# Decode attention on one core: scores and maxima by unit instead of by pair, and two more kept loads

## The chip, the cores and the metric

The kernel runs on one core of a Trainium2 chip. The core has a matrix engine (PE, with its weight loads listed apart as PEld), a vector engine (DVE), a scalar engine (ACT), GpSimd (POOL) and a sync engine (SP), which here issues nearly all DMAs. The engines run their own instruction lists in order and wait for each other on semaphores. The metric is the device time of one execution in microseconds.

## The reference

Two layers run twice over one token for each of four batches: attention over a cache of 4096 keys, then a gated feed-forward layer.

```python
x = x + A(layernorm(x))   # attention
x = x + B(layernorm(x))   # gated feed-forward
x = x + A(layernorm(x))   # the same weights and caches again
x = x + B(layernorm(x))

# A: q = x @ wq, 32 heads of 128; 8 key/value heads, each shared by 4 query heads
scores = q . k * 128**-0.5          # [4, 32, 1, 4096]
o = softmax(scores) . v
A = o.reshape(4, 1, 4096) @ wo      # to 512
# B: (sigmoid(x @ w_gate) * (x @ w_up)) @ w_down, F = 1792
```

All inputs are bfloat16. K and V are 4 x 8 blocks of 4096 x 128, 1.0486 MB each, 64 blocks in all, and both attention passes read all of them.

## The kernel before

A *unit* is one layer, batch and key/value head: 64 units, and each needs its K and its V block. Two units next to each other in head number make a *pair*, 32 in all. ORDER lists the pairs (layer, batch, pair of heads). Batches go their own way: when a batch's four pairs of layer 0 are done, its feed-forward and its next query are computed in a *pass* of 17 short steps (pass_steps), spread between the work on other batches' pairs.

Blocks live in 12 slots of SBUF; the four quarters of wq become slots 13 to 16 once the last query is made. KEPT names, per batch, the units whose K (ahead of the slash) and V (behind it) stay in their slots from layer 0 to layer 1. All others are loaded twice. Before, 27 blocks are kept, so 101 K and V loads remain of 128. LOADS is the order in which SP issues the loads (k, v, and the weight parts o, g, u, d). The function pump issues the next load whenever a slot is free on the list; SP's DMA then waits for the last reader of that slot.

PROGRAM is the order of all other work, written out by hand, a letter for each step. The letters that matter here, for pair g:

- t, T: turn half or all of a K block in place on DVE (k_turn, L1014)
- b: POOL copies the pair's queries into qz (q_blocks, L728)
- s, z: the scores on PE (scores, L1016 to L1040), in two parts
- m: maxima over each row on DVE (smax, L1049)
- p: PE spreads the row maxima to all rows (spread_max, L1057)
- n: DVE picks each row's own maximum (bias, L1068)
- e: the exponential on ACT (expo, L1080); h: POOL splits the sums in a high and a low half (L1109, L1112)
- P: PE transposes the probabilities (ptrans, L1098); C, D: eight copies to pT, on ACT (L1150; for the last pair half on DVE, L1142)
- r, i: row sums on PE (L1164) and their reciprocals on DVE (L1176)
- a: half a unit's PV product (pv, L1196); the second half gives the V slot back
- o, N: normalise (L1227); w: product with wo (L1253, L1279 or L1346)
- x: a row sum of one wo part on ACT (wo_row_sums, L602); X, Y: the last layer norm's preparation (Y is rows_before, L1393)
- a dot: the next step of the pass of a batch

Each engine's list has the steps in this order, so a step whose input is late holds up everything behind it on that engine. A pair's scores lie in one PSUM bank of 128 rows by 512 columns. The array's four strips of 32 output rows each take one of two units and one of two halves of the keys:

```python
r0 = 64 * ul + 32 * c
S_ps[p][r0:r0 + 4 * REP, :]   # ul: unit of the pair, c: half
rhs=ktv[ul][:, :, c, :, b2, :, e_]   # 512 columns
```

Part s has the first two of four contraction steps t for both units, part z the other two; both K slots go back after z.

Of the kernel before, what the change touches and what calls it, by code (L numbers as in the profile page):

```python
# [5 lines left out]
dt = mybir.dt  # L6
ACTF = mybir.ActivationFunctionType
ALU = mybir.AluOpType
# [126 lines left out]
stzxaamatbpaoCnwfitaDTaewFl sazamhrPpCoDwnei.....w..Ph..r.aa...aa.oiC.Daa..b sxTzmpnaebaTowtPChr  # L135
sziampnbDatweaahtPr sCzobimDaap snzaamewhPCobp swtrznftehwiDrtFabalmaaotwxtPp
sxinw.zCmbaTp.eD.w.ha.TnaaPo. sCDrz.iawTePbma..hpa.aCnTo.r..DiT sz.aw.bmae.P.apaohDrtw
swinCewahazPabmapC strznoeiamwpbhnDaParaoiC sDewfaazFPhlaarwmpConiwaDtt.aTehabPawoC.DTri.
swz.w..mawa.ap.baTn soezhrimP.p.bTCa.Daw.nt.aa.. se.ztw.Pbw smzCphnoribDtweaPtmaahpaC
snerzmDoiaaTpaabhnwTP sCorzwwettwbiaDaawmpTPhaCDr sToinzbmepwahPanraaTC  # L140
sDwoeziambPpahaaroCnDiwteahfrFtaalaPDoiw.T.CTaa. szmw...pb.Tn.eaa.
shzr.oPwwDiw..C.matpwa.n.eP..tabTa shzDomCbrpnei szahmawPaTrbaCp snDoizmaehabPapawrCtw
stonzmbwiapTDenhPaa sDraozeCiaPhamCrapaDnowwefihFPDCaaaalorXaaYiNawa
# [3 lines left out]
def bass_interleave_layers__gqa_block_cached__glu_gated_glu__decode_kernel(  # L147
# [60 lines left out]
    valid_p = wide_sb[:, 0:NV]  # L208
    pe_sb = wide_sb[:, NV:NV + 4 * P]
    mask_f = wide_sb[:, NV + 4 * P:2 * NV + 4 * P].rearrange("p (n w) -> p n w", n=8)  # L210
# [4 lines left out]
    pT_sb = sbt([P, 2, 4, 2, 4, REP], dt.bfloat16, "pT")  # L215
    NSMALL = 87
# [20 lines left out]
    rm_bf = small(2, dtype=dt.bfloat16)[:, 0:1]  # L237
    hl_bf = small(2, dtype=dt.bfloat16)
    head_bf = small(2 * REP, dtype=dt.bfloat16)
    eye4 = small(Bn)  # L240
    sel_bf = small(Bn, dtype=dt.bfloat16)
    sm_sb = small(1)
    nm_sb = small(1)
    head_f = small(2 * REP)
# [24 lines left out]
    ident_f = t_row[:, 0:P]  # L269
    half_f = t_row[:, P:P + 8 * REP].rearrange("p (u w) -> p u w", u=2)  # L270
# [164 lines left out]
    act(lambda e: e.activation(ident_f[:, :], ident_bf[:, :], ACTF.Copy), reads=IDENT, writes=["ra"])  # L435
    rows_f = ident_f.rearrange("p (u c w) -> p u c w", u=2, c=2)
# [4 lines left out]
    def head_masks():  # L441
        for u in range(2):
            dve(
                (lambda u: lambda e: e.tensor_copy(
                    valid_p.rearrange("p (c a u h) -> p u c a h", c=2, a=4, u=2)[:, u],
                    rows_f[:, u, :, 0:4 * REP].rearrange("p c (a h) -> p c a h", h=REP),
                ))(u),
                reads=["ra"],
                writes=[f"valid{u}"],
            )  # L450
        dve(
            lambda e: e.tensor_tensor(
                half_f[:, :, :], rows_f[:, :, 0, 0:4 * REP], rows_f[:, :, 1, 0:4 * REP], ALU.add
            ),
# [3 lines left out]
            lambda e: e.tensor_reduce(  # L458
                head_f.rearrange("p (u h) -> p u h", u=2),
                half_f.rearrange("p u (a h) -> p u h a", h=REP),  # L460
                AX.X,
                ALU.add,
            ),
# [13 lines left out]
        dve(lambda e: e.tensor_copy(sel_bf, eye4), reads=["eye4"], writes=["sel"])  # L477
        dve(
            lambda e: e.tensor_scalar(
                mask_f, head_f.unsqueeze(1).broadcast_to([P, 8, 2 * REP]), 1.0, BIG, op0=ALU.subtract, op1=ALU.mult  # L480
            ),
            reads=["head"],
            writes=["mask"],
        )
        dve(lambda e: e.tensor_reduce(rm_sb, head_f, AX.X, ALU.add), reads=["head"], writes=["rm"])
# [530 lines left out]
    def scores(g, part):  # L1016
        l, b, _ = seq[2 * g]
        p = g % 2
        ktv, rd = [], list(QZ)
        for ul in range(2):  # L1020
            st = where["kt", b, seq[2 * g + ul][2]]
            ktv.append(slot[st].rearrange("p (x c j t k e) -> p x c j t k e", x=XJ, c=2, j=4, t=2, e=2))
            rd.append(f"s{st}")
        fns = []
        for t in range(2 * part, 2 * part + 2):
            b2, e_ = divmod(t, 2)
            for ul in range(2):
                for c in range(2):
                    r0 = 64 * ul + 32 * c
                    fns.append(  # L1030
                        (lambda t, b2, e_, c, r0, ul: lambda e: e.matmul(  # L1031
                            S_ps[p][r0:r0 + 4 * REP, :],
                            lhsT=qz_sb[:, ul, t, :, :].rearrange("p a r -> p (a r)"),
                            rhs=ktv[ul][:, :, c, :, b2, :, e_].rearrange("p x j k -> p j x k"),
                            start=(t == 0),
                            stop=(t == NT4 - 1),
                        ))(t, b2, e_, c, r0, ul)
                    )
        if part == 0:
            S.group("pe", fns, reads=rd, writes=[f"S{p}"])  # L1040
            return
        S.last_write[f"S{p}"] = S.group("pe", fns, reads=rd)
# [10 lines left out]
    def spread_max(g, n):  # L1053
        ms_bank[0] = n
        S.inst(
            "pe",
            lambda e: e.matmul(  # L1057
                O_ps[n][:, 128:128 + 16 * REP], lhsT=rm_bf.broadcast_to([P, P]), rhs=valid_p[:, :],
                start=True, stop=True,
            ),  # L1060
            reads=["rmb", "valid0", "valid1"],
            writes=[f"O{n}"],
        )

    def bias(g):
        n = ms_bank[0]
        dve(
            lambda e: e.tensor_tensor_reduce(  # L1068
                O_ps[n][:, 256:256 + 16 * REP], O_ps[n][:, 128:128 + 16 * REP],
                mask_f.rearrange("p n w -> p (n w)"),  # L1070
                rowk_f, BIG, ALU.add, ALU.min, nm_sb,
            ),
            reads=["mask", "rowk"],
            writes=[f"O{n}", "nm"],
        )

    def expo(g):
        p = g % 2
        act(
            lambda e: e.activation(  # L1080
                pe_sb,
                S_ps[p][:, :],
                ACTF.Exp,
                bias=nm_sb,
                scale=exp_scale,
                accum_out=sm_sb,
            ),
            reads=[f"S{p}", "nm"],
            writes=["pe0", "sm"],
        )  # L1090
# [591 lines left out]
```

## Time and profile before

| What | Before |
|---|---|
| Median of 3 runs | 310.94 us (310.31 to 311.24) |
| Profiled execution, its own time | 309.33 us |
| Its span, first to last instruction | 307.3 us |
| Busy: PE, PE weight loads, DVE, ACT, POOL | 219.4, 130.2, 183.7, 107.3, 40.6 us |
| Mean granted TensorE clock | 0.684 |
| Read from HBM | 119.80 MB, 390 GB/s over the span |
| K and V loads | 101 blocks, one of them in two halves |
| Stream transposes of K (L1014) | 103.8 us on DVE in the main slots |
| Scores (L1031) | 496 + 16 matmuls, 60.9 + 2.1 us |
| PV (L1196), main group | 1824 matmuls, 60.2 us |

The profile page divides the span in 40 slices of 7.7 us and gives the busy share of each engine in tenths. Rows by line give busy time, mean time of one instruction, and the idle time ahead of it with what ended it. The chain of waits goes back from the last instruction to what released it at each step.

### The profile page before, as it was taken

What the parts mean: (1) busy time and instruction counts of PE and PEld (TensorE: products, weight loads), DVE (VectorE), ACT (ScalarE), POOL (GpSimd) and SP (SyncE); (2) the same over time, 40 slices, a digit from 0 to 9 for tenths busy, and PEclk for the clock granted to TensorE, in tenths of its full rate; (3) what the DMA queues carried; (4) which work ended last, traced back from release to release, by engine and by line L of the source; (5) the groups of instructions that cost most, each with busy time, mean ns of one, the idle gap of its engine ahead of it and who ended that gap; (6) DMA issues with size and microseconds to landing.
All of it is one profiled execution on the core that took longest, in us unless ns stands there. A gap on an engine that the chain in (4) does not pass through costs nothing.

```text
span 307.3 us, 10060 instructions
## 1 busy us (share of the span) xinstructions
PE 219.4 (71%) x4264; PEld 130.2 (42%) x4264; DVE 183.7 (60%) x407; ACT 107.3 (35%) x350; POOL 40.6 (13%) x205
## 2 busy tenths in 40 slices
PE   1223334544889699798979987965965689799986
PEld 1221112212545343556445735443433645355575
DVE  6345665437333767686933586766974496767333
ACT  2001123134213254624345632343555204446700
POOL 0002110101000212111111020131112010222000
PEclk9999999999995555557655557575755575555555
DMA  7999999999999999999999999999999999999940
GB/s 278 424 398 403 403 410 399 412 422 421 397 409 419 414 401 395 424 417 419 419 416 405 422 419 419 419 420 419 419 421 416 422 361 358 423 424 418 420 166 5
DMA packets 20788, 120.45 MB, mean 392 GB/s; under 512 B 1924, under 2 KB 6024, under 8 KB 7688
## 3 DMA queue, kind: packets, MB, share of 16 engines
q1 hardware_dynamic: 20720, 119.81, 95.8%
q8 instruction: 34, 0.56, 0.7%
q14 instruction: 10, 0.08, 0.1%
q10 hardware_dynamic: 24, 0.01, 0.0%
HBM read 119.80 MB, written 0.00 MB: 390 GB/s over the span
## 4 chain that ended last, share of the span: by engine, by line
DMA 41%; PE 33%; DVE 12%; SPq 5%; issue 4%; ACT 2%; POOL 1%; DVEq 0%; ACTq 0%; POOLq 0%
DMA slot<-in_A_v_cache_dram 33%; PE S_ps L1031 10%; PE O_ps L1196 9%; DMA slot<-in_A_k_cache_dram 8%; DVE slot L1014 7%; SPq L372 5%; PE M_ps L904 4%; PE PT L1098 2%; DVE small L1049 1%; ACT pT L1150 1%; PE AC L1253 1%; POOL qz L728 1%; PE M_ps L953 1%; PE M_ps L504 1%; PE O_ps L1346 1%
## 5 line engine op out<-in xcount | busy, mean ns | idle before, releaser
L1014 DVE STREAM_TRANSPOSE slot<-slot 128x1024 f32<-128x1024 f32 (+1 forms) x61 | 103.8, 1707 | 22.5 <-DMA slot<-in_A_k_cache_dram 20.1
L1150 ACT ACTIVATE pT<-PT 32x128 bf16<-32x128 f32 x236 | 63.3, 268 | 78.2 <-PE PT L1098 34.6
L1196 PEld LDWEIGHTS O_ps<-pT,slot 128*128 128x128 bf16 x1824 | 55.5, 104 | 50.1 <-DMA slot<-in_A_v_cache_dram 15.5
L1196 PE MATMUL O_ps<-pT,slot 128*128 128x4 bf16 x1824 | 60.2, 166 | 22.3 <-DMA slot<-in_A_v_cache_dram 14.5
L1031 PE MATMUL S_ps<-slot,qz 128*16 128x512 bf16 x496 | 60.9, 610 | 18.7 <-DVE slot L1014 11.3
L728 POOL COPY qz<-qs 32x32 bf16<-32x32 bf16 x128 | 26.2, 205 | 123.3 <-PE S_ps L1031 65.6
L1049 DVE TENSOR_REDUCE small<-S_ps 128x1 bf16<-128x512 f32 x32 | 21.8, 681 | 25.1 <-PE S_ps L1031 25.1
L1080 ACT ACTIVATE wide<-S_ps,small 128x512 bf16<-128x512 f32 x32 | 22.0, 687 | 38.7 <-DVE small L1068 21.5
L1031 PEld LDWEIGHTS S_ps<-slot,qz 128*16 128x16 bf16 x496 | 11.1, 102 | 36.1 <-DVE slot L1014 13.8
L1098 PE MATMUL PT<-ident_bf,wide 128*128 128x64 bf16 (+1 forms) x288 | 18.3, 225 | 2.9 <-ACT pT L1150 2.9
L1098 PEld LDWEIGHTS PT<-ident_bf,wide 128*128 128x128 bf16 x288 | 14.9, 120 | 8.2 <-ACT pT L1150 3.0
L1109 POOL CAST small<-small 128x1 bf16<-128x1 f32 x32 | 6.0, 187 | 80.9 <-ACT wide L1080 66.7
L904 PE MATMUL M_ps<-wq,small 128*1 128x512 bf16 x128 | 15.5, 602 | 0.0
L1068 DVE CUSTOM_DVE_ANT_0 O_ps<-O_ps,wide,small 128x64 f32<-128x64 f32 x32 | 8.9, 278 | 9.2 <-PE O_ps L1057 5.1
L1057 PE MATMUL O_ps<-wide,small 128*128 128x64 bf16 x32 | 7.1, 221 | 10.1 <-DVE small L1049 9.7
L1227 DVE TENSOR_TENSOR oT<-O_ps,small 128x8 bf16<-128x8 f32 (+1 forms) x32 | 5.3, 164 | 14.7 <-PE O_ps L1196 12.3
L1253 PE MATMUL AC<-wo,oT 128*1 128x512 bf16 x96 | 12.0, 596 | 0.8 <-DVE oT L1227 0.8
L713 ACT ACTIVATE qs<-M_ps 128x128 bf16<-128x128 f32 x8 | 1.9, 280 | 27.2 <-PE M_ps L702 27.2
L1057 PEld LDWEIGHTS O_ps<-wide,small 128*128 128x128 bf16 x32 | 3.3, 104 | 16.4 <-DVE small L1049 15.8
L1164 PEld LDWEIGHTS O_ps<-small 128*128 128x128 bf16 x62 | 4.2, 109 | 12.0 <-issue 6.0
L858 PE MATMUL M_ps<-wu,small 128*1 128x512 bf16 (+1 forms) x64 | 8.9, 522 | 0.0
L919 ACT ACTIVATE t_row<-M_ps,small 128x512 bf16<-128x512 f32 x4 | 2.7, 687 | 15.6 <-PE M_ps L904 8.4
(143 smaller groups left out, 204.9 us busy)
## 6 DMA issues: line engine op xcount, KB each, us to landing
slot<-in_A_v_cache_dram SPq DMA_DIRECT2D x52, 1024.0 KB, 9.9
slot<-in_A_k_cache_dram SPq DMA_DIRECT2D x44, 1024.0 KB, 10.5
wq<-in_A_wq_dram SPq DMA_DIRECT2D x2, 2048.0 KB, 10.2
wo<-in_A_wo_dram SPq DMA_DIRECT2D x8, 512.0 KB, 17.6
wq<-in_A_v_cache_dram SPq DMA_DIRECT2D x2, 1024.0 KB, 10.3
wq<-in_A_k_cache_dram SPq DMA_DIRECT2D x2, 1024.0 KB, 14.4
wg<-in_B_w_gate_dram SPq DMA_DIRECT2D x2, 896.0 KB, 14.6
wu<-in_B_w_up_dram SPq DMA_DIRECT2D x2, 896.0 KB, 13.3
```

The costliest lines, as they stand in the source:

```text
L372: "sp", (lambda dst, frm: lambda e: e.dma_start(dst, frm))(dst, frm), sem, writes=[key], deps=deps
L728: (lambda a, ps: lambda e: e.tensor_copy(qz_sb[ps, :, :, a, :], qs_sb[b][ps, :, u * REP:(u + 2) * REP].rearrange("p t (u r) -> p u t r", r ...
L904: (lambda k, st: lambda e: e.matmul(M_ps[h][32 * st:32 * st + 1, :], lhsT=xc_bf[:, k, 0:1], rhs=wv[:, k, h, :, st, :], start=(k == 0), sto ...
L1014: dve(lambda e: e.transpose(kf, kf), writes=[f"s{st}"])
L1031: (lambda t, b2, e_, c, r0, ul: lambda e: e.matmul(S_ps[p][r0:r0 + 4 * REP, :], lhsT=qz_sb[:, ul, t, :, :].rearrange("p a r -> p (a r)"), ...
L1049: dve(lambda e: e.tensor_reduce(rm_bf, S_ps[p][:, :], AX.X, ALU.max), reads=[f"S{p}"], writes=["rmb"])
L1057: lambda e: e.matmul(O_ps[n][:, 128:128 + 16 * REP], lhsT=rm_bf.broadcast_to([P, P]), rhs=valid_p[:, :], start=True, stop=True,),
L1080: lambda e: e.activation(pe_sb, S_ps[p][:, :], ACTF.Exp, bias=nm_sb, scale=exp_scale, accum_out=sm_sb,),
L1098: (lambda w, a0, a1, c0: lambda e: e.matmul(PT[:, c0:c0 + 16 * (a1 - a0)], lhsT=wide_sb[:, NV + 64 * w:NV + 64 * w + P], rhs=valid_bf[:, : ...
L1150: (lambda dst, frm: lambda e: e.activation(dst, frm, ACTF.Copy))(dst, frm),
L1196: (lambda n, x, c, j: lambda e: e.matmul(bank[:, ul * REP:(ul + 1) * REP], lhsT=vv[:, x * JG + c * 4 + j, :], rhs=pT[:, x % 2, j, x // 2, ...
L1253: (lambda r, h, i: lambda e: e.matmul(AC[32 * r:32 * r + 1, :], lhsT=oT_sb[:, h, own_column:own_column + 1], rhs=wo_sb[:, h, :], start=(j ...
```

## The change

- The score matmuls go unit by unit. The four strips take four quarters of one unit's keys (c and x1), the bank's left 256 columns are the first unit and the right 256 the second. Part s is now all of the first unit, part z all of the second: 16 matmuls of 256 columns each, where each part had 8 of 512.
- A K slot is given back after its own unit's part.
- Each row's maxima, exponentials and sums are made per unit: one reduction with two results, two spreading matmuls, a scalar_tensor_tensor and a minimum reduction in place of one fused operation, two exponentials of 256 columns, four row-sum matmuls for two.
- The masks that serve these are built another way at the start (head_masks), and the layouts of pT and small tiles follow.
- KEPT has 29 blocks, and ORDER, LOADS and PROGRAM are written anew.

```diff
-KEPT = ["012345/23", "0145/45", "167/167", "23567/26"]
+KEPT = ["012345/23", "0145/01", "167/0167", "23567/236"]
 ORDER = """
-000 002 001 003 011 013 101 010 012 100 102 022 021 020 023 112 110 103 030 032 123 120 033 031 113
-111 121 133 131 130 132 122
+002 000 003 001 013 011 101 012 010 100 102 022 021 020 023 110 112 030 103 032 123 120 033 031 111
+113 121 131 133 130 132 122
 """
 LOADS = """
-vkkookokgk kookkvovko vgkkvvkvvo uuddvvvkvk kkvvkvvkvk kvvkvkkvvk vvvvvvkkkk vvvkvkvkvk kvvkkkvkvv
-kvvkvkkvkv kvkvvvkkvv vvvvv
+ookokokkvk koovvkkgkk vkovvkovvg uuddvvvkkv kkkvvvvkvk kvvkvkvkvk vvvvvvkkvk vkvvkkkvkv kvvkkkvkvv
+vkkvvkkvvv kvkkkvkvvv vvv
 """
 PROGRAM = """
-tw szmpnbetT szhrmTbiTPwpDn sezhCttmaaptaatnrPCoiDb seazmhpwtabrawPwntaehotDCPwir
...
-stonzmbwiapTDenhPaa sDraozeCiaPhamCrapaDnowwefihFPDCaaaalorXaaYiNawa
+stzbmpntt szxmethxwTptb strPiCznaDaeaaoPmxwpDnhrCTTib swazemhaaaoPrttbpTDwniC
...
+saCDareoiPzhaaramaCpwDonewfiFaPwwahCwlaXYaarDoiawNawa
 """
...
     def scores(g, part):
-        l, b, _ = seq[2 * g]
+        l, b, u = seq[2 * g + part]
...
+        half = slice(256 * part, 256 * part + 256)
         fns = []
-        for t in range(2 * part, 2 * part + 2):
+        for t in range(NT4):
             b2, e_ = divmod(t, 2)
-            for ul in range(2):
-                for c in range(2):
-                    r0 = 64 * ul + 32 * c
+            for c in range(2):
+                for x1 in range(2):
+                    r0 = 64 * c + 32 * x1
...
-                            S_ps[p][r0:r0 + 4 * REP, :],
-                            lhsT=qz_sb[:, ul, t, :, :].rearrange("p a r -> p (a r)"),
-                            rhs=ktv[ul][:, :, c, :, b2, :, e_].rearrange("p x j k -> p j x k"),
+                            S_ps[p][r0:r0 + 4 * REP, half],
+                            lhsT=qz_sb[:, part, t, :, :].rearrange("p a r -> p (a r)"),
+                            rhs=ktv[:, 2 * x1:2 * x1 + 2, c, :, b2, :, e_].rearrange("p x j k -> p j x k"),
...
-        for i in (2 * g, 2 * g + 1):
-            if l == 1 or not kept("k", i):
-                free.append(where.pop(("kt", b, seq[i][2])))
+        if l == 1 or not kept("k", 2 * g + part):
+            free.append(where.pop(("kt", b, u)))
 
     def smax(g):
-        dve(lambda e: e.tensor_reduce(rm_bf, S_ps[p][:, :], AX.X, ALU.max), reads=[f"S{p}"], writes=["rmb"])
+        dve(lambda e: e.tensor_reduce(rm_bf, S_ps[p].rearrange("p (u n) -> p u n", u=2), AX.X, ALU.max), reads=[f"S{p}"], writes=["rmb"])
...
     def spread_max(g, n):
-            lambda e: e.matmul(
-                O_ps[n][:, 128:128 + 16 * REP], lhsT=rm_bf.broadcast_to([P, P]), rhs=valid_p[:, :],
+                (lambda u: lambda e: e.matmul(
+                    O_ps[n][:, P + 64 * u:P + 64 * u + 64], lhsT=rm_bf[:, u:u + 1].broadcast_to([P, P]), rhs=valid_bf,
...
     def bias(g):
-            lambda e: e.tensor_tensor_reduce(
-                O_ps[n][:, 256:256 + 16 * REP], O_ps[n][:, 128:128 + 16 * REP],
-                mask_f.rearrange("p n w -> p (n w)"),
-                rowk_f, BIG, ALU.add, ALU.min, nm_sb,
+            lambda e: e.scalar_tensor_tensor(
+                out=shifted, in0=maxima, scalar=rowk_f, in1=mask_f.rearrange("p n w -> p (n w)").unsqueeze(1).broadcast_to([P, 2, 64]),
+                op0=ALU.mult, op1=ALU.add,
...
+        dve(lambda e: e.tensor_reduce(nm_sb, shifted, AX.X, ALU.min), reads=[f"O{n}"], writes=["nm"])
 
     def expo(g):
-                pe_sb,
-                S_ps[p][:, :],
+        for u in range(2):
+                    pe_sb[:, half],
+                    S_ps[p][:, half],
...
     def row_sums(g):
-                    bank[:, 16:16 + 2 * REP], lhsT=hl_bf[:, n:n + 1].broadcast_to([P, P]), rhs=head_bf,
+                    bank[:, 16 + u * REP:16 + (u + 1) * REP], lhsT=hl_bf[:, n, u:u + 1].broadcast_to([P, P]), rhs=head_bf,
```

More of the change, by code (lines that the diff above doesn't have):

```diff
@@ L1054, in spread_max @@
         ms_bank[0] = n
[L1055 removed]
+        S.group(
             "pe",
[L1057 to L1061 removed]
+            [
+                (lambda u: lambda e: e.matmul(
+                    O_ps[n][:, P + 64 * u:P + 64 * u + 64], lhsT=rm_bf[:, u:u + 1].broadcast_to([P, P]), rhs=valid_bf,
+                    start=True, stop=True,
+                ))(u)
+                for u in range(2)
+            ],
+            reads=["rmb"] + IDENT,
             writes=[f"O{n}"],
```

126 lines of the change are left out of this document (54 added, 72 removed).

## The prediction

> **What bounds the kernel now.** I read the page's 40 slices first, then the queues, then busy time and DMA rate stretch by stretch, then the chain of waits, and last the rows of the operations that the diff touches.
>
> ```profile
> PE   1223334544889699798979987965965689799986
> DMA  7999999999999999999999999999999999999940
> GB/s 278 424 398 403 403 410 399 412 422 421 397 409 419 414 401 395 424 417 419 419 416 405 422 419 419 419 420 419 419 421 416 422 361 358 423 424 418 420 166 5
> q1 hardware_dynamic: 20720, 119.81, 95.8%
> DMA 41%; PE 33%; DVE 12%; SPq 5%; issue 4%; ACT 2%; POOL 1%; DVEq 0%; ACTq 0%; POOLq 0%
> ```
>
> The DMA engines are full from the first slice to the 38th, near 420 GB/s, and stop about 12 us before the end. PE fills nine tenths of many slices in the second half too, so it is the second limit.
>
> ```profile
> 112.00:120.00 8.00, 7.96 (x146) 4.38 (x147) 4.05 (x9) 3.47 (x13) 2.12 (x11) 0.50 0.97 376
> 164.00:168.00 4.00, 4.00 (x92) 2.67 (x92) 1.20 (x5) 2.27 (x8) 1.20 (x6) 0.50 0.99 399
> 244.00:252.00 8.00, 6.20 (x87) 3.27 (x87) 7.33 (x14) 1.34 (x4) 1.06 (x5) 0.65 0.95 365
> 256.00:260.00 4.00, 3.79 (x39) 1.83 (x31) 2.09 (x13) 2.08 (x8) 0.31 (x2) 0.50 0.88 309
> ...
> 266.40:292.20 25.80, 23.82 (x452) 13.34 (x452) 15.82 (x33) 15.87 (x54) 5.57 (x29) 0.50 1.01 421
> ```
>
> Columns: stretch, length, busy PE, PE weight loads, DVE, ACT, POOL, granted clock, DMA share, GB/s. In the first four rows compute is late in giving slots back and the queue runs short. Against 420 GB/s they lose (44x8 + 21x4 + 55x8 + 111x4)/420 = 3.1 us. In the last row the queue is full while PE idles 2.0 us of 25.8.
>
> ```profile
> 228.38 12.18 DMA slot<-in_A_v_cache_dram
> ...
> 240.61 0.59 PE O_ps L1196 x16
> ...
> 272.38 22.35 DMA slot<-in_A_v_cache_dram
> ...
> 294.87 0.99 PE O_ps L1196 x32
> 295.86 0.60 PE S_ps L1393 x16
> ```
>
> This is the chain in order of time (start, length). It ends on the last V loads: all are queued by 275, the last lands at 294.7, and 12.4 us of compute follow. So the end is bytes over rate, plus a tail.
>
> **The change, part by part.**
>
> *Two loads fewer.* The kept lists hold 27 units before and 29 after (a V each of batches 2 and 3 more), so 101 K and V loads become 99. A load is 1.0486 MB: at 420 GB/s 2.50 us, together **-5.0 us**. Where in the list? Counted from the two load lists, 22 loads stand behind the last layer-0 V in both. The saving lies ahead of it, so the last batch's pass (its serial feed-forward and query, which that V releases: 240.6 to about 266 here) may start 5 us earlier, and what follows has the same length. That matters since PE has only 2.0 us to spare behind the pass. The gain holds if compute ahead of it keeps up: from 104 to 244 PE is busy 115.9 of 140 us, and 24 idle minus 5 leaves 19. Bounds 0 and -5.0; I take -5.0.
>
> *Slots given back.* A K slot now goes back after its own unit's scores, not the pair's; but more kept units leave fewer slots in circulation. I walked both programs through the slot count, taking for each load the bytes between it and the newest load that the steps up to its release need. The smallest distance was 1.0 MB before, at the first of the loads that are issued from 246 to 257 us, with others of 2.1. After, the smallest is 2.1 MB (5.0 us); between them stand mostly 3.1 to 5.2 MB in both. Bounds: all 3.1 us recovered, or as much lost again if steps lie otherwise than counted; nearer to a small gain, **-0.5 us**.
>
> *Scores.* Sixteen matmuls of 512 columns per pair, in four strips, become 32 of 256.
>
> ```profile
> L1031 PE MATMUL S_ps<-slot,qz 128*16 128x512 bf16 x496 | 60.9, 610 | 18.7 <-DVE slot L1014 11.3 <-POOL qz L728 4.4 <-DVE oT L1227 1.8
> L833 PE MATMUL M_ps<-wg,small 128*1 128x256 bf16 x16 | 4.5, 408 | 0.0
> L1608 PE MATMUL S_ps<-wd,t_row 128*4 128x128 bf16 x56 | 1.7, 309 | 0.2 <-DVE t_row L785 0.2
> L1068 DVE CUSTOM_DVE_ANT_0 O_ps<-O_ps,wide,small 128x64 f32<-128x64 f32 x32 | 8.9, 278 | 9.2 <-PE O_ps L1057 5.1 <-ACT slot L1150 1.7 <-PE O_ps L1164 1.6
> L1068 DVE DVE_READ_ACCUMULATOR2_ANT small<- 128x1 f32 x32 | 4.5, 141 | 0.0
> L1080 ACT ACTIVATE wide<-S_ps,small 128x512 bf16<-128x512 f32 x32 | 22.0, 687 | 38.7 <-DVE small L1068 21.5 <-PE PT L1098 6.9 <-issue 5.2
> L1080 ACT ACTIVATION_READ_ACCUMULATOR wide<-S_ps,small 128x1 f32 x32 | 6.2, 193 | 0.0
> ```
>
> A sequence of 16 takes 1.89 us: four sets of four strips at a pitch of (1.89-0.61)/3 = 0.43 us. The only four-strip row with narrower matmuls, L1608 (128 columns), has (1.69-0.31)/13 = 0.106 us per set. That is a quarter, so pitch goes with columns: 256 take 0.21, and eight sets 7x0.21 + 0.41 = 1.88 us. Bounds: 0 per pair, and +1.71 if a set of 256 takes as long as one of 512. I take 0, by the L1608 row.
> The Trainium skill speaks against the split: "TensorEngine Tiling (Array Packing)", section Instruction Overhead, gives each matmul about 60 cycles on trn2; at 1.2 GHz ("TensorE: Matmul & The Clock Gate", What's actually happening) an estimate of 50 ns, 0.8 us more per pair if it adds. L1608's 30 ns per matmul disagrees with an addition; as a floor it doesn't bind.
>
> *Softmax chain, per pair.* The fused bias operation (0.28, its accumulator read ending 0.35 us after the start) becomes a scalar_tensor_tensor over 128 columns (between 168 ns at 4 columns and 688 at 512: 0.29) and a minimum (158 and 681: 0.29). With a gap of 0.05 that is +0.28. The exponential becomes two of 256 columns (between 280 ns at 128 and 687 at 512: 0.42), each with a 0.19 read: 1.22 for 0.88, +0.34. A second max-spreading matmul is 0.05, by nine transposes in 0.45. Together +0.67 us. Two more row-sum matmuls (0.1) lie beside it. POOL's two copies of sums stay two, one column wider. Queued behind these are PE's transposes, ACT's eight copies of P, and so the PV matmuls that give V slots back. On all 32 pairs that would be 21 us; on the chain of waits the exponential stands twice and the bias operation four times, 2x0.34 + 4x0.28 = 1.8 us, each time with a wait for a load later that absorbs it. Bounds -1.2 (unit 0's scores begin a half K turn, 1.24 us, earlier) and +1.8 us; **0**, with the V loads as cover.
>
> *Start.* Two wo loads go ahead of the first K and V0 behind: K0 still lands after 6.3 MB, K1 after 0.5 MB more (1.2 us). Two of the four wo row sums (0.63 + 0.19 us each) now stand on ACT ahead of the first exponential, and need the sixth wo part, behind 14.7 MB, so landing near 38 us. The exponential ran at 30.1, so it and pairs 0 and 1 slip about 9 us. The first load that needs a returned slot then stands behind 20.8 MB, near 53 us, and its release (pair 2's scores) comes by about 43: covered by 10 us of queued loads, **0**. Without that cover the slip would count in full. POOL's query copies wait for the same scores. In head_masks an ACT copy and three DVE copies go, one memset comes, all under the wq loads: 0.
>
> *Tail.* The 16 matmuls of L1393 (0.60 us, on the chain between the last V landing and the end) now stand ahead of the last two units' PV. A row-sum group takes the place, 0.2 us by the L1164 steps of 0.15. **-0.4**; bounds -0.6 and +0.2.
>
> Sum: 309.33 (span 307.3 and 2.0 around it) - 5.0 - 0.5 - 0.4 = 303.4 for the profiled execution. It lay 1.6 below the median of 310.94, so 305.0 is the median.
>
> **The rivals.**
> 1. *Gain given back behind the last pass.* If that pass doesn't start earlier, the rest can shrink only by PE's 2.0 us idle and its last waits for V, about 1 us: 308. For it: PE at 92% there. Against: equal load counts behind the last layer-0 V.
> 2. *Softmax chain on the path: slower.* If it sets the pace in 14 pairs, +9.4: 314.4. It decides from 5.9/0.67 = 9 pairs on. For it: row 112 to 120, PE full and the queue short. Against: six pairs on the chain now, four of them before 111 us.
> 3. *Score sets don't halve.* +1.71 per pair: seven pairs after 244, where PE idles 5.5 us of 48, give 12.0 - 5.5 = +6.5; sixteen from 104 to 244 give 27.4 against 19, +8.4: 305.0 + 14.9, 320. The 0.8 us worked out from the skill's page would stay under 19 in the first stretch and pass 5.5 by 0.1 in the second: 305.1, no case of its own.
> 4. *Loads don't set the pace*, so two fewer change nothing: 311. Against: the chain's last 22 us.
>
> **How the numbers follow.** Forecast 0.56 (own range 302.5 to 306.5), rival 1 0.16, rival 2 0.14, rival 3 0.08, rival 4 0.06. A difference under 0.3% (0.9 us) can't be told from none here. Faster 0.56 + 0.16 = 0.72, same 0.06, slower 0.14 + 0.08 = 0.22. The range runs from 302, where most of the 3.1 us is recovered, to 313, below rival 2's centre: out are rival 3, about half of rival 2 and 0.04 below.
>
> **What would show it.** Queue q1 at 117.7 MB; the last V landing near 289 with about 12 us behind it; 32 score matmuls in 1.9 us per unit pair; exponentials near 0.42 us; no stretch below 350 GB/s after 20 us. The prediction is wrong if DMA shows gaps from 104 to 260, if the last PV waits for PE's own work and not for a load, or if the score pitch per set is well over 0.21 us.

## The result, and the profile after

The changed kernel takes 307.98 us (median of 6 runs, 307.71 to 309.48) against 310.28 for the kernel before beside it (6 runs, 309.27 to 311.24): ratio 0.994, interval 0.9911 to 0.997. A second set gives 308.21 against 309.85, ratio 0.9943 (0.9907 to 0.9979). So the change gains 1.6 to 2.3 us where 5.9 were forecast. (Below, one run of the changed kernel with half V loads and three of the changed kernel with limited loads lay more than 1.5% above the fastest of the same kernel, and are left out of the times and ratios.)

The profiled execution of the first set was its slowest, 309.48 us with a span of 307.6. That of the second set took 307.05 with a span of 305.1. Sums below name the one they use.

Page of the changed kernel, first set: busy time by engine, slices, queues, chain by engine.

```profile
PE 218.7 (71%) x4872; PEld 148.5 (48%) x4872; DVE 191.8 (62%) x401; ACT 117.7 (38%) x413; POOL 40.5 (13%) x205
PE   1223325555879689779779987964788799799986
GB/s 292 395 393 420 395 422 419 407 415 406 408 410 419 416 419 323 411 419 420 419 417 392 422 348 423 420 409 413 422 412 422 393 354 391 381 422 423 412 96 3
q1 hardware_dynamic: 20432, 117.71, 95.0%
q8 instruction: 38, 0.62, 0.8%
PE 5%; DVE 2%; issue 0%; ACT 0%; DVEq 0%
```

Queue q1 has the 2.1 MB less that were counted (119.81 before). The rate has new dents, 323 and 348 GB/s, that the row of before does not have, beside the old one in slices 33 to 35. The last line can't be compared with the one before (DMA 41%): this chain was followed back to 283 us only, where that of before goes back to the start. The chain of the second set is whole and has DMA 30%, with its last wait for a load over at 263.1 us, where that of before waits until 294.7.

Its stretches with a weak queue (columns as in the prediction):

```profile
116.00:120.00 4.00, 3.97 (x99) 2.97 (x99) 2.61 (x5) 2.96 (x11) 0.71 (x4) 0.50 0.91 334
120.00:124.00 4.00, 3.83 (x83) 2.34 (x80) 3.34 (x7) 3.72 (x13) 0.93 (x6) 0.52 0.97 307
176.00:180.00 4.00, 3.15 (x76) 2.34 (x73) 3.85 (x5) 0.15 (x1) 0.41 (x2) 0.50 0.99 336
244.00:248.00 4.00, 4.00 (x56) 2.06 (x48) 3.72 (x12) 0.10 (x1) 0.23 (x2) 0.50 0.91 330
260.00:264.00 4.00, 2.49 (x82) 2.04 (x78) 1.57 (x5) 2.40 (x10) 0.55 (x3) 0.93 0.99 340
```

In the first two and the fourth PE is full or nearly so: compute is late and slots come back late. Adding (420 - rate) x 4 / 420 over all 4 us stretches below 420 GB/s from 40 to 288 us, the queue is short by 5.1 us in the kernel before, 8.8 in the changed one, and 6.8 in its second set. So 1.7 to 3.7 of the 5.0 us that two loads save are lost again as gaps in the queue. It shows in the PV of the last layer-0 V, which releases the last batch's pass: here are its rows in the kernel before, the changed kernel and the second set.

```profile
240.61 0.59 PE L1196 MATMUL O_ps<-pT,slot 128*128 128x4 bf16 x16 [1.38 <-DMA slot<-in_A_v_cache_dram]
```

```profile
238.82 0.99 PE L1182 MATMUL O_ps<-pT,slot 128*128 128x4 bf16 x32
```

```profile
237.13 1.01 PE L1182 MATMUL O_ps<-pT,slot 128*128 128x4 bf16 x32
```

It starts 1.8 and 3.5 us earlier than before, not 5, and PE no longer waits there for the load.

Now the part behind the last batch's pass, taken to begin with the transposes of the last query (L702 before, L684 after), which end the pass: the kernel before, the changed kernel, and the changed kernel's second set, each from these transposes to the end of the span.

```profile
264.71:307.30 42.59, 35.98 (x862) 24.22 (x862) 22.73 (x64) 16.99 (x58) 6.38 (x32) 0.50 0.73 300
```

```profile
262.64:307.60 44.96, 37.98 (x987) 28.53 (x984) 25.57 (x66) 19.77 (x72) 6.34 (x32) 0.51 0.71 286
```

```profile
260.30:305.10 44.80, 37.67 (x987) 28.43 (x984) 25.77 (x66) 19.73 (x72) 6.33 (x32) 0.53 0.72 296
```

In the second set the pass ends 4.4 us earlier than before, and what follows is 2.2 us longer; -2.2 us is the whole difference of the spans. The rest grew because PE has 1.7 to 2.0 us more work there, with its idle time nearly as before (6.6, 7.0 and 7.1 us). By lines, changed kernel (first set) less kernel before: scores 10.56 - 9.60, transposes of the probabilities 3.70 - 3.00 (one group of nine more), row sums 1.50 - 1.21, spreading matmuls 1.36 - 1.09, PV 13.83 - 13.66: together +2.4, and some small groups less. PE's busy time over the whole span has not grown (219.4 before, 218.7 and 219.4 in the two sets), so this is work that the new order puts behind the pass instead of ahead of it.

The chain of the changed kernel (first set) in order of time, near its end:

```profile
291.17 0.52 PE O_ps L1182 x16
291.69 0.46 PE PT L1084 x9
292.15 0.02 issue
292.18 0.27 ACT pT L1136
...
294.76 0.53 PE S_ps L1379 x14
295.29 0.94 PE O_ps L1182 x32
296.23 0.11 PE M_ps L1150 x4
296.34 0.43 PE O_ps L1182 x16
```

Where the chain of before waited 22.35 us for the last V loads, this one runs through PE's own work and ACT's copies. The V that the chain of before ended on, that of unit 62, lands at 294.1 by the trace's landing records, and PE gets to it only at 295.67, after other work:

```profile
295.67 0.57 PE L1182 MATMUL O_ps<-pT,slot 128*128 128x4 bf16 x16
```

### The profile page after: what moved, and what is told of

Same layout as the page of the kernel before. It is cut to its first block, busy times and chain, and to the rows that moved or that the text cites. A ratio compares the mean times of both kernels' runs of the same rounds, so it can differ in the third digit from the quotient of the medians.

```text
span 307.6 us, 11306 instructions
## 1 busy us (share of the span) xinstructions
PE 218.7 (71%) x4872; PEld 148.5 (48%) x4872; DVE 191.8 (62%) x401; ACT 117.7 (38%) x413; POOL 40.5 (13%) x205
## 5 line engine op out<-in xcount | busy, mean ns | idle before, releaser
L996 DVE STREAM_TRANSPOSE slot<-slot 128x2048 f32<-128x2048 f32 (+1 forms) x55 | 100.1, 1831 | 19.2 <-DMA slot<-in_A_k_cache_dram 18.7
L1012 PE MATMUL S_ps<-slot,qz 128*16 128x256 bf16 x976 | 59.2, 396 | 24.3 <-POOL qz L710 13.3
L1182 PEld LDWEIGHTS O_ps<-pT,slot 128*128 128x128 bf16 x1856 | 55.2, 103 | 32.8 <-ACT pT L1136 11.1
L1012 PEld LDWEIGHTS S_ps<-slot,qz 128*16 128x16 bf16 x976 | 26.5, 112 | 46.0 <-DVE slot L996 12.8
L1066 ACT ACTIVATE wide<-S_ps,small 128x256 bf16<-128x256 f32 x64 | 30.3, 474 | 39.6 <-DVE small L1059 16.0
L1029 DVE TENSOR_REDUCE small<-S_ps 128x2 bf16<-128x512 f32 x32 | 21.8, 681 | 19.5 <-PE S_ps L1012 19.5
L1095 POOL CAST small<-small 128x2 bf16<-128x2 f32 x32 | 5.9, 185 | 115.6 <-ACT wide L1066 89.2
L1052 DVE SCALAR_TENSOR_TENSOR O_ps<-O_ps,small,wide 128x128 f32<-128x128 f32 x32 | 11.0, 345 | 8.5 <-PE O_ps L1038 7.0
L1066 ACT ACTIVATION_READ_ACCUMULATOR wide<-S_ps,small 128x1 f32 x64 | 12.3, 193 | 0.0
L1059 DVE TENSOR_REDUCE small<-O_ps 128x2 f32<-128x128 f32 x32 | 9.3, 292 | 3.2 <-ACT wide L1066 0.4
L1038 PE MATMUL O_ps<-ident_bf,small 128*128 128x64 bf16 x64 | 8.5, 225 | 3.3 <-DVE small L1029 3.2
L1038 PEld LDWEIGHTS O_ps<-ident_bf,small 128*128 128x128 bf16 x64 | 4.1, 105 | 11.1 <-DVE small L1029 10.0
```

What stands on the lines that cost most here:

```text
L996: dve(lambda e: e.transpose(kf, kf), writes=[f"s{st}"])
L1012: (lambda t, b2, e_, c, x1, r0: lambda e: e.matmul(S_ps[p][r0:r0 + 4 * REP, half], lhsT=qz_sb[:, part, t, :, :].rearrange("p a r -> p (a r)"),
L1029: dve(lambda e: e.tensor_reduce(rm_bf, S_ps[p].rearrange("p (u n) -> p u n", u=2), AX.X, ALU.max), reads=[f"S{p}"], writes=["rmb"])
L1038: (lambda u: lambda e: e.matmul(O_ps[n][:, P + 64 * u:P + 64 * u + 64], lhsT=rm_bf[:, u:u + 1].broadcast_to([P, P]), rhs=valid_bf, start=T ...
L1052: lambda e: e.scalar_tensor_tensor(out=shifted, in0=maxima, scalar=rowk_f, in1=mask_f.rearrange("p n w -> p (n w)").unsqueeze(1).broadcast ...
L1066: (lambda u, half: lambda e: e.activation(pe_sb[:, half], S_ps[p][:, half], ACTF.Exp, bias=nm_sb[:, u:u + 1], scale=exp_scale, accum_out=s ...
```

## The experiments

The expectations name theories by letters. Those that the text takes up: **A**, the longer softmax chain eats the gain; **B**, slots come back too late, so the kept blocks cost what their loads save; **D**, behind the last pass compute sets the end; **F**, PE stands while a block of its instruction list is fetched. **G**, those stops are chance, or no part of what sets the end. C (the loads were never the gain) and E (the last loads set the end) missed wherever they differed from the others. Ratios stand against the kernel before in runs on the same chip.

### The kept blocks by themselves

The new order with the 27 blocks kept as before in batches 2 and 3. The two V loads that this brings back were put where they are needed (the first for layer 1 of batch 2, the second for layer 1 of batch 3):

```diff
-KEPT = ["012345/23", "0145/01", "167/0167", "23567/236"]
+KEPT = ["012345/23", "0145/01", "167/167", "23567/26"]
-... kvvkkkvkvv vkkvvkkvvv kvkkkvkvvv vvv
+... kvvkkkvvkvv vkkvvkkvvv kvvkkkvkvvv vvv
```

> The changed kernel with the two additional kept V blocks given up again (27 kept, two V loads more, each put into the list of loads where its turn was; all else as in the changed kernel). Theory A, longer softmax steps per pair eat the gain: the loads are worth their full 5.0 us, so this is 308.0 + 5.0 = 313, ratio to before 1.009. Theory B, two more kept blocks leave too few slots in circulation, and the queue runs dry for 4 us more: those 4 us come back against the 5.0 of the loads, so 309, ratio 0.996. Theory C, the gain was never in the loads (compute sets the pace): 308, ratio 0.993.

Measured: 310.12 us against 310.08, ratio 0.9993 (0.9973 to 1.0014). All of the change but the keeping is worth nothing, and the two kept blocks bring about 2 us, not 5.0. B came nearest, with 309. In this kernel's trace the last pass ends at 262.4 us, 2.3 earlier than before, and the part behind it takes 45.8 us for 42.6, with PE busy for 38.2: the longer end belongs to the new order and not to the two blocks.

The old order with the two more kept, and their loads taken out:

```diff
-KEPT = ["012345/23", "0145/45", "167/167", "23567/26"]
+KEPT = ["012345/23", "0145/45", "167/0167", "23567/236"]
```

> The kernel before with the same two V blocks kept in addition (29 kept, two V loads taken out of the list; scores, softmax and order as before). Theory A: the full 5.0 us are gained, 305.3, ratio 0.984. Theory B: the queue runs dry as in the changed kernel, 308 or more, ratio 0.993 or more. Theory C: 310, ratio 1.00.

Measured: 315.16 us, ratio 1.0161 (1.0138 to 1.0184). Two loads fewer make the old order 5.1 us slower. Its stretches from 248 to 260 us:

```profile
248.00:252.00 4.00, 4.00 (x63) 2.08 (x63) 3.79 (x9) 0.00 (x0) 0.51 (x3) 0.50 0.70 229
252.00:256.00 4.00, 2.78 (x49) 1.38 (x43) 2.99 (x5) 0.69 (x1) 0.30 (x2) 0.87 1.01 399
256.00:260.00 4.00, 2.69 (x72) 2.08 (x76) 1.65 (x4) 0.78 (x2) 0.38 (x2) 0.56 0.64 227
```

The queue runs dry: short by 14.0 us over 40 to 288 where the kernel before is short by 5.1, and 8.9 less the 5.0 saved is most of the loss. This is B, in the old order. The new order can afford the kept blocks, at a part of their price.

Which of the two brings it? The new order with only the V of batch 2 given up, and with only that of batch 3:

```diff
-"167/0167", "23567/236"
+"167/167", "23567/236"
```

> The changed kernel with the additional V block of batch 2 given up (28 kept); its second load stands ahead of the last layer-0 V. If the gain comes through an earlier last pass, this block is what brings it: 310, ratio 1.000. If slots ahead of the pass are what is short: 307.5, ratio 0.992.

```diff
-"167/0167", "23567/236"
+"167/0167", "23567/26"
```

> The changed kernel with the additional V block of batch 3 given up (28 kept); its second load stands behind the last layer-0 V, where compute sets the end. If so the load costs nothing there and the slot is free for longer ahead: 307.5 to 308, ratio 0.992 to 0.994. If the loads behind the pass count: 310, ratio 1.000.

Measured: without the V of batch 2 309.80 us, ratio 0.9992 (0.9972 to 1.0012), the whole gain gone; without that of batch 3 307.22, ratio 0.9899 (0.9875 to 0.9924), as fast as the changed kernel or 0.8 us faster. That last difference is small against the intervals (0.994 has 0.9911 to 0.997). So one block does all of it. The second load of the V of batch 2 stands ahead of the last layer-0 V in the list, and without it the pass starts earlier. The PV of that last V, first in the kernel that loads the V of batch 2 again, then in the one that loads that of batch 3 again:

```profile
240.25 1.02 PE L1182 MATMUL O_ps<-pT,slot 128*128 128x4 bf16 x32 [1.21 <-DMA slot<-in_A_v_cache_dram]
```

```profile
237.13 1.02 PE L1182 MATMUL O_ps<-pT,slot 128*128 128x4 bf16 x32
```

The second load of the V of batch 3 stands behind, where compute sets the end. The kernel with it, from 240 to 268 us:

```profile
240.00:268.00 28.00, 22.95 (x499) 15.32 (x500) 20.90 (x47) 10.97 (x38) 4.51 (x22) 0.72 1.01 410
```

The changed kernel (first set) in the same stretch:

```profile
240.00:268.00 28.00, 23.88 (x460) 15.16 (x461) 19.23 (x45) 8.68 (x30) 4.28 (x21) 0.62 0.99 375
```

One slot more in circulation, and the weak stretch there is gone (410 for 375 GB/s): the load that it costs is won back. The sums short of 420 GB/s from 240 to 268 are 0.67 us here, and 3.00 and 2.07 in the two sets of the changed kernel.

### The softmax chain

The changed kernel with one maximum over the row, one spreading matmul, the fused bias and one exponential of 512 columns; and the kernel before with the steps as long as in the changed one.

```diff
-rm_bf, S_ps[p].rearrange("p (u n) -> p u n", u=2), AX.X, ALU.max
+rm_bf[:, 0:1], S_ps[p][:, :], AX.X, ALU.max
...
-scalar_tensor_tensor(...)
-tensor_reduce(nm_sb, shifted, AX.X, ALU.min)
+tensor_tensor_reduce(..., rowk_f, BIG, ALU.add, ALU.min, nm_sb[:, 0:1])
...
-for u in range(2): activation(pe_sb[:, half], S_ps[p][:, half], ...)
+activation(pe_sb, S_ps[p][:, :], ...)
```

> The changed kernel with scores by unit, but the softmax steps of the kernel before: one maximum over the whole row, one spreading matmul, the fused bias operation, one exponential of 512 columns. The sums of the two units are then no longer kept apart (one sum over both, the other a constant), which is left out of the computation. Theory A: 0.7 to 0.8 us less in each of 32 chains, and the last stretch shorter: 304 to 305, ratio 0.981. Theory B and C: 307.5 to 308, ratio 0.993.

```diff
-tensor_tensor_reduce(...)
+scalar_tensor_tensor(...)
+tensor_reduce(nm_sb, O_ps[n][:, 2 * P:3 * P], AX.X, ALU.min)
...
-activation(pe_sb, S_ps[p][:, :], ..., accum_out=sm_sb)
+for u in range(2): activation(pe_sb[:, half], S_ps[p][:, half], ..., accum_out=(sm_sb, sm2_sb)[u])
```

> The kernel before with only its softmax steps made as long as in the changed kernel: two spreading matmuls, a scalar_tensor_tensor over 128 columns and a minimum, two exponentials of 256 columns each with its accumulator read (the second half's sum is left out of the computation). Theory A: the queue runs dry in more places and the last stretch grows, 313 to 314, ratio 1.010. Theory B and C: under 1 us, 310.3 to 311, ratio 1.001.

Measured: joined again 307.81 us, ratio 0.9929 (0.9906 to 0.9952), no difference from the changed kernel that can be told. Lengthened in the old order 312.05, ratio 1.0058 (1.0033 to 1.0083): +2.0 us. So A holds half: in the old order the longer chain is paid, in the new one taking it away brings nothing at the end. In the joined kernel's trace the PV of the last layer-0 V starts at 235.61 us, 1.5 to 3.2 earlier than in the two sets of the changed kernel, but PE then idles 1.59, 1.70 and 0.85 us where it waits for nothing that the trace shows (see F), and the span is 306.5, within the two sets' 305.1 to 307.6. PE of the joined kernel inside the pass:

```profile
249.35 0.65 PE L936 MATMUL M_ps<-t_row,wd 128*128 128x1 bf16 x19
251.58 0.29 PE L936 MATMUL M_ps<-t_row,wd 128*128 128x1 bf16 x5 [1.59 <-issue]
```

A sequence of 24 like matmuls, whose inputs are all there, is cut by 1.59 us.

### Slots by the pair, and half V loads at the end

Both K slots given back only after the second unit's scores:

```diff
-if l == 1 or not kept("k", 2 * g + part):
-    free.append(where.pop(("kt", b, u)))
+if part == 1:
+    for i in (2 * g, 2 * g + 1): ...
```

> The changed kernel, but both K slots of a pair are given back after the pair's second part, as before; all else is the same. Theory B, slots in circulation decide: loads are issued later wherever the first unit's slot was the one waited for, the queue runs dry for 2 to 5 us more: 310 to 313, ratio 1.000 to 1.010. If the return by unit is worth nothing: 308, ratio 0.993.

Measured: 307.72 us, ratio 0.9919 (0.9881 to 0.9957). B's 310 to 313 did not come: in this order the earlier return of a K slot is worth nothing.

V loads of the units 58 to 62 cut to half, in both kernels: 5 x 0.52 MB, 6.2 us of queue at 420 GB/s, all near the end.

```diff
+if kind == "v" and 58 <= n <= 62:
+    q = NJ * DH // 2
+    parts = [(slot[s][:, 0:q], src[:, 0:q], f"d{s}", f"s{s}")]
```

> The changed kernel with five of the last six V loads (those of units 58 to 62) cut to half a block, 2.6 MB or 6.2 us of transfer less; the other half is what the slot held before, so the attention of these units is left incomplete. Theory D, behind the last pass compute sets the end: at most 1 us less, 307, ratio 0.990. Theory E, the last loads set the end: 301.8, ratio 0.973.

> The kernel before with the same five V loads cut to half a block. Its PE waited 0.24 + 0.71 + 0.32 us for V loads near the end. Theory D: about 1.3 us less and no more, 309.0, ratio 0.996. Theory E: 304, ratio 0.980.

Measured: changed 307.48 us, ratio 0.9928 (0.9894 to 0.9962), by the ratios 0.5 below the changed kernel, which can't be told from none; before 308.43, ratio 0.995 (0.993 to 0.997), 1.4 less. If the last loads set the end, both would have lost up to 6.2 us. This shows D, and for the kernel before too: its chain of waits ended on V loads, yet with those loads half as long it could give up only 1.4 us.

The changed kernel once more, for a trace nearer its median:

> The changed kernel once more, for a profile nearer to its median (the first profiled execution lay 1.5 us above it): 308.0, ratio 0.993, with the last V landing about 1 us earlier than in the first profile (294.2) and the queue short by 7 to 9 us between 40 and 288.

Its numbers stand in the section above: 308.21 us, the pass over at 260.30, and 44.80 us behind it.

### The split of the scores, and PE's list

The kernel before, its score matmuls cut in two of 256 columns, with the same slots, loads and order:

```diff
-for t in range(2 * part, 2 * part + 2):
+half = slice(256 * part, 256 * part + 256)
+for t in range(NT4):
...
-S_ps[p][r0:r0 + 4 * REP, :],
+S_ps[p][r0:r0 + 4 * REP, half],
...
-rhs=ktv[ul][:, :, c, :, b2, :, e_]...
+rhs=ktv[ul][:, 2 * part:2 * part + 2, c, :, b2, :, e_]...
```

> The kernel before with its score matmuls cut in two of 256 columns (the first part takes the left half of the bank, the second the right; same result, same bytes, same order, 1024 more entries in PE's list). Theory F, PE's own instructions arrive late: the gaps of 0.7 to 1.6 us that PE shows behind the last pass in the changed kernel all fall on the same place in a block of 256 entries of its list, so they are the reload of its list behind full data queues, and more entries per microsecond bring them here too: 1 to 2 us longer, 311 to 312, ratio 1.004, with gaps at block ends. Theory G, those gaps are chance: 310, ratio 1.000.

Measured: 313.48 us, ratio 1.0106 (1.0071 to 1.0142): +3.5 us. The scores' own rows, in this kernel:

```profile
L1032 PE MATMUL S_ps<-slot,qz 128*16 128x256 bf16 x992 | 59.7, 399 | 19.7 <-DVE slot L1014 12.8 <-POOL qz L728 4.6 <-DVE oT L1228 1.6
L1032 PEld LDWEIGHTS S_ps<-slot,qz 128*16 128x16 bf16 x992 | 27.8, 114 | 37.8 <-DVE slot L1014 16.6 <-POOL qz L728 5.4 <-DVE oT L1228 2.6
```

The matmuls take 59.7 us where 496 of 512 columns took 60.9: the pitch halves. But there are twice as many weight loads (27.8 us busy for 11.1), and the list of PE is some 1,000 entries longer. What a longer list can bring is seen in PE's timeline of this kernel:

```profile
127.53 0.51 PE L1099 MATMUL PT<-ident_bf,wide 128*128 128x32 bf16 x7
130.25 0.26 PE L1099 MATMUL PT<-ident_bf,wide 128*128 128x64 bf16 x2 [2.21 <-issue]
```

Nine transposes with their input there, cut after seven for 2.21 us. The trace has the answer in the instruction queue: its packets of 16 KB come once per 256 entries of PE, which are its matmuls, its weight loads and some 140 waits in all (34 for 8,669 recorded entries before, 38 for 9,890 after, 38 for 9,693 here). From 60 us on, each idle time of PE over 1.1 us that any trace here marks "issue" stands at the end of such a block; some shorter ones don't (0.92 us at 88.5 in the kernel before). Worked out from the traces' records (us; a stop is counted from the start of the last entry of a block to the start of the next, so up to 0.4 us longer than the idle time that the timelines show):

```
kernel                 PE passes the end   next packet   PE's stop at the end
                       of the block ahead  starts        of the block
changed                262.2               266.5         267.4, for 1.38
changed                267.4               272.5         274.1, for 0.82
before, scores split   122.1               127.8         127.8, for 2.45
```

From 45 to 290 us, in the traces of the kernel before, the changed kernel (both sets) and the two kernels with split scores of this section, half of the block ends without a stop have their packet 2.9 to 3.8 us after the block ahead is used up; at the stops marked "issue" it comes 3.5 to 6.9 us after, and PE has used the block in 4.0 to 8.1 us. Blocks used in under 5.6 us without a stop had their packet within some 3 us. From 297 us on, with next to no data under way, it comes 0.6 to 1.7 us after, and blocks used in 3.6 to 4.1 us bring no stop. So, in these traces, PE stands where the packet comes late and the block is soon used up. The sum of stops at block ends over 0.3 us is 1.6 us before, 6.7 and 9.2 in the two sets of the changed kernel, and 6.7 here. (Some of it is ordinary waits that fall there.) If F is so, the stops follow the list and not the work. So the same kernel with 64 more matmuls, read by nothing, early where PE is idle: the block ends move 128 entries forward.

```diff
+if nb == Bn:
+    S.group("pe", [lambda e: e.matmul(M_ps[0][:, 0:4], lhsT=ident_bf, rhs=ident_bf[:, 0:4], ...) for _ in range(64)], ...)
```

> The kernel before with split score matmuls, and 64 matmuls that nobody reads put into PE's idle time before 26 us, so that every block end of its list falls 128 entries earlier in the program. Theory F: the gaps stand again at entry 192 of each block of 256, so at other places of the program than 82.6, 127.8, 192.4 and 293.5; their sum may differ by 2 us, so 311 to 315. Theory G (the place decides): gaps at the same matmuls as without the shift, 313.5.

Measured: 312.29 us, ratio 1.006 (1.0036 to 1.0083). The stop at 127.8 is gone and others of 2.07, 2.40, 1.19, 2.00 and 1.31 us stand at 145.1, 177.4, 232.3, 288.0 and 295.1. The first of them in this kernel's timeline:

```profile
144.72 0.57 PE L1209 MATMUL O_ps<-pT,slot 128*128 128x4 bf16 x16
147.19 0.59 PE L588 MATMUL M_ps<-t_row,small 128*128 128x4 f32 x2 [1.91 <-issue]
```

That shows where the stops lie, not what they cost: their sum is 12.5 us here and 6.7 without the shift, while this kernel is not the slower of the two (1.006 against 1.0106). A stop counts only where PE is on the path.

Can the stops be shortened? The packet shares the DMA engines with the data (the page counts q1 and q8 as shares of the same 16). If it is late because they are full, fewer loads in flight should bring it earlier: each load from the 40th on waits until the third one ahead of it has landed.

```diff
+if total - len(loads) > 40:
+    deps = deps + [landed[-3]]
```

> The changed kernel with at most three K or V loads on the way at any time (each waits for the landing of the third before it), so that behind the last pass not six loads stand ahead of whatever else needs the DMA engines. Theory F: PE's gaps at block ends behind the last pass go, 1.5 us shorter, 306.5, ratio 0.988. Theory G: no change, or a little longer as the queue is shorter: 308 to 309, ratio 0.994 to 0.997.

> The kernel before with the same limit of three loads on the way. It shows no gap at a block end behind the last pass, so theory F and theory G both expect 310 to 311, ratio 1.000 to 1.003.

> The changed kernel with the joined softmax steps of the earlier run (sums of the two units not kept apart) and the limit of three loads on the way. In that run PE stood 1.75, 1.86 and 1.02 us at block ends from 249 on. Theory F: these go, and the shorter softmax steps show at last: 304 to 305, ratio 0.982. Theory G: 308, ratio 0.993.

Measured: changed 309.49 us, ratio 0.9979 (0.9949 to 1.0009); before 311.05, 1.0022 (0.9995 to 1.0049); joined 307.92, 0.9949 (0.9921 to 0.9978). The gains that F expected (306.5 and 304 to 305) did not come; G's 308 is what the joined kernel took. The changed kernel came out 1.2 us longer than without the limit, by ratios whose intervals overlap. The stops from 262 to 290 us of the changed kernel went away, but from 190 to 240, where it moved 417 GB/s, the limited one moves less:

```profile
190.00:240.00 50.00, 38.30 (x883) 26.34 (x881) 35.64 (x61) 24.30 (x88) 8.01 (x40) 0.57 1.00 393
```

So the limit was put on the last 15 loads alone (`> 98` for `> 40`):

> The changed kernel with the limit of three loads on the way only for the last 15 loads, which are issued behind the last pass; ahead of it nothing is changed. Theory F, late reloads of PE's list: the gaps from 262 to 295 go as with the general limit (there 1.38, 0.82 and 0.18 became none), and the queue ahead stays as it was: 306.5, ratio 0.989. Theory G, the gaps are no part of what sets the end: 308, ratio 0.994.

Measured: 308.12 us, ratio 0.9921 (0.9891 to 0.9951), the changed kernel's own time, as G expected and not F's 306.5. PE's timeline of this kernel at the two old places and at a new one:

```profile
265.70 0.39 PE L1020 MATMUL S_ps<-slot,qz 128*16 128x256 bf16 x3
266.54 1.86 PE L1020 MATMUL S_ps<-slot,qz 128*16 128x256 bf16 x29 [0.45 <-issue]
...
293.85 0.40 PE L1340 MATMUL O_ps<-oT,wo 128*128 128x4 bf16 x9
296.19 0.33 PE L1340 MATMUL O_ps<-oT,wo 128*128 128x4 bf16 x7 [1.94 <-issue]
```

The stop at 267 shrank from 1.00 to 0.45 us and that at 274 is gone, but one of 1.94 us, close to the end, took their place. Shifting refuted G as far as it calls the stops chance; these runs don't refute it as to the end. What F costs the changed kernel as a whole stays open: that the stops exist and move with the list is shown, that removing them all would bring back the missing 3 us is not.

## Why the prediction was right or wrong

*Loads, -5.0: wrong in size.* The bytes are right. Two steps failed. First, that the pass would start 5 us earlier: the PV of the last layer-0 V starts 1.8 us (first set) or 3.5 us (second) earlier, about what the queue's further gaps of 3.7 and 1.7 us leave of 5.0. Second, and more surely, "what follows has the same length": it grew by 2.2 to 2.4 us, and by 3.2 in the new order with 27 blocks kept. I had noted that PE had "only 2.0 us to spare" there and counted loads on both sides of the last layer-0 V, but not PE's work behind it, which the new order raised from 35.98 to 37.98 us (37.67 in the second set). That this work decides there, and not the loads, is shown by the half V loads. The two kept blocks are worth about 2 us, and one of them all of it.

*Slots, -0.5: wrong.* The queue lost 1.7 to 3.7 us by the sums above, around the upper bound of +3.1. My walk gave the distance in bytes between a load and the load that its release needs; it left out how late compute runs. Counted from the traces (bytes issued less bytes landed, at each issue), the load that was the walk's smallest of before, 1.0 MB, was issued with 0.54 MB outstanding; in the changed kernel a load with a distance of 4.2 MB, at 117.3 us, was issued with the same 0.54. Nine loads are issued with under 1 MB outstanding there, before two. Returning K by unit, which I took for the cause of a small gain, brings nothing.

*Scores, 0: right for the pitch, and not for what else the split costs.* The pitch, on which I argued, was right: 32 of 256 columns in 1.88 us.

```profile
264.38 1.88 PE L1012 MATMUL S_ps<-slot,qz 128*16 128x256 bf16 x32 [0.57 <-POOL qz L710]
```

The Trainium skill's overhead per matmul ("TensorEngine Tiling (Array Packing)", Instruction Overhead) would as an addition have made this 2.7 us by the estimate in the prediction; the trace disagrees with an addition. Yet the split by itself costs the old order 3.5 us. I counted execution times and not entries: the 1,000 more of them stand in PE's list, and I had no row for what fetching a list costs. That the list makes up the 3.5 us is not shown: with the shift the stops grew and the time did not, and the weight loads' 27.8 us for 11.1 are a rival that no run takes apart. In the changed kernel the share is not measured apart.

*Softmax, 0: right here, but not for my reason.* The durations came out a little higher than I estimated.

```profile
L1066 ACT ACTIVATE wide<-S_ps,small 128x256 bf16<-128x256 f32 x64 | 30.3, 474 | 39.6 <-DVE small L1059 16.0
L1052 DVE SCALAR_TENSOR_TENSOR O_ps<-O_ps,small,wide 128x128 f32<-128x128 f32 x32 | 11.0, 345 | 8.5 <-PE O_ps L1038 7.0
L1059 DVE TENSOR_REDUCE small<-O_ps 128x2 f32<-128x128 f32 x32 | 9.3, 292 | 3.2 <-ACT wide L1066 0.4
```

That is 0.474, 0.345 and 0.292 us for 0.42, 0.29 and 0.29. The V loads were the cover that I named; in the old order it doesn't hold, and the longer chain costs 2.0 us, just above my upper bound of +1.8. In the new order joining it again changes the time by 0.2, because what it gains ahead of the pass is lost within it and behind it.

*Start, 0: right.* The first exponential slipped from 30.1 to 41.4 us, 11 where 9 were reckoned, and the queue stayed full: from 40 to 104 us it moved 413 GB/s, short by 1.07 us, and before 412, short by 1.22.

*Tail, -0.4: right for the stretch, not for the path.* From PE's start on the V of unit 62 to the end it is 11.9 us in both sets, 12.4 before. But the forecast counted from that V's landing (294.7 before, which I called the last; two halves of one more V follow it), and from there it is 13.4 to 13.5 us: PE reaches this V late, and the 16 matmuls moved ahead of it are part of what makes it late. So the end gains nothing by them.

*The rivals.* The first named the place, behind the last pass, and its 308 is the time; but its condition, that the pass doesn't start earlier, was not met, so the number agrees by luck. Two of the signs named as making the forecast wrong did come: the last PV waits for PE's own work, and the queue has gaps from 104 to 260 us. The second, softmax on the path, holds in the old order only. The third, score sets that don't halve, is refuted by the pitch, though the split had another cost. The fourth, loads that don't set the pace, holds behind the last pass and not ahead of it.

A sum in the old order's terms: split matmuls +3.5, longer softmax +2.0, and the new order without further keeping back at the old time. If these add up in the new order as well, its order, load list and other parts make up about 5.4 us, by subtraction and not by a run; the joined kernel, which gains nothing in the new order, speaks against a plain sum. Then 2 us come from one kept block.

## What to carry to other kernels

In this kernel a saved load was worth time only ahead of the step that the queue releases, and the one saved behind it brought nothing: list each saved load by which side of the last such step it stands on, and compare the busy time of the bounding engine behind that step in both orders, not the number of loads. Count entries as well as execution time when an instruction is split, and keep a block only if the slot that it takes is not needed where the queue is weakest: the same two blocks cost 5.1 us in one order and brought 2 in the other. The shortest time here is that with one of them kept, 307.22 us, though it isn't clearly apart from the changed kernel's 308.

## What was not expected of the hardware

PE's instruction list arrives in 16 KB packets of 256 entries, through the instruction queue. While the data queue is full, each mostly starts 2.9 to 3.8 us after the block ahead was used up, but 3.5 to 6.9 us at the stops, and nearly all are 0.9 to 1.2 us long. PE stops, with nothing to wait for in the profile but "issue", where it has used up a block before its next packet is there: idle for up to 2.2 us at once. A change of 64 matmuls early on moves these stops to other places; the two kernels that differ by this took 312.29 and 313.48 us, though their intervals overlap.

A lower granted clock is not what the split scores cost. In the kernel before with split scores it was 1.00 from 104 to 130 us, where the kernel before has 0.50, and over the whole span 0.778 for 0.684, and yet the former was the slower. These are their rows, first with split scores, then before:

```profile
104.00:130.00 26.00, 21.39 (x474) 14.03 (x462) 18.05 (x35) 11.50 (x37) 5.61 (x28) 1.00 0.99 391
```

```profile
104.00:130.00 26.00, 22.67 (x411) 12.62 (x411) 18.12 (x37) 13.44 (x44) 5.29 (x27) 0.50 1.00 407
```
